# Attention products of a linear-attention and MLP kernel moved from half-array to quarter-array tiles

## The chip, the cores and the metric

The kernel runs on one core of one Trainium2 chip. The metric is device time in microseconds (us) of one execution. Every time quoted is the median of several executions of the fast state, except for two single looks (a_run, b_run32), which are called so and whose state is unknown. TensorE is called PE below, with PEld for its weight loads. VectorE is DVE, ScalarE is ACT, GpSimd is POOL, and SyncE is SP.

## The reference

A linear attention with a decaying state runs over 768 steps, for 4 batches of 8 heads of width 48. Its output, as rows of 8 x 48 = 384, goes through a layer norm and an MLP of 384 to 1536 to 384 with a residual.

```python
for t in range(S):                                    # S = 768
    cur = np.einsum('bhd,bhe->bhde', u[None] * kt, vt)
    y[:, :, t] = np.einsum('bhd,bhde->bhe', rt, state + cur)
    state = wt[:, :, :, None] * state + np.einsum('bhd,bhe->bhde', kt, vt)
x = y.transpose(0, 2, 1, 3).reshape(B, S, H * D)      # 4 x 768 x 384
xn = (x - mu) / np.sqrt(var + 1e-06) * g_ln
out = x + np.maximum(xn @ w_ch1, 0.0) @ w_ch2         # 384 -> 1536 -> 384
```

Everything is float32, except the two MLP weights, which come as float64 words that the kernel unpacks itself.

## The kernel before

The kernel works in units of two heads of one batch, 16 units in all, two units per round. Time is cut into chunks of 64 steps, and two chunks sit side by side on the 128 partitions. Within a chunk the products of R and K are built in six levels: at level `lev` only pairs of blocks of `2**lev` steps meet, and K and R are then scaled by the decays before the next level. Three kinds of product concern us: `a_ps` (R times K), `kv` (K times v, which gives the states) and `y` (A times v plus R times state). Each used the 128 rows of the array and half of its columns. To keep two heads or two chunks apart within the rows, one operand was padded with zeros (`pad`, `vz`, `s_pad`).

```python
    def right_half(q, lev):              # ACT copies R's right halves into a padded tile
        ...
        for j in range(2):
            rows = ds(HP * j, HP)
            ACT.copy(
                out=pad[rows, j, :].rearrange("p (q n) -> p q n", n=n), in_=R[rows, :, 1, :]
            )

    def level(qs, lev):
        ...
        for q in qs:
            ps = got[q] = ps_a.tile([P, NC, 2, C // 2], F32, tag="a", ...)
            for c in range(NC):
                for i in range(2):
                    m = 2 * c + i
                    PE.matmul(
                        ps[ds(C * i, C), c], st[q]["k"][:, ts(m, C)], pad[:, :, ts(m, C // 2)],
                        start=True, stop=True,
                    )
        for q in qs:
            ...   # POOL scales K, DVE scales R, then right_half(q, lev + 1) on ACT
        for q in qs:
            ...   # DVE copies the products into A under a mask
```

The MLP of a finished batch is a generator of 52 steps per batch; the schedule hands out its steps between the attention levels at a pace `RATE`.

```python
    RATE = 1.05 * MLP_STEPS * 2 / (G * NLEV)
    for rnd in range(NS + 1):
        now, old, new = ...              # the units of this round, the last and the next
        for lev in range(NLEV):
            if now:
                level(now, lev)
            if lev in (2, 3):
                for q in old[lev - 2 : lev - 1]:
                    outputs(q)
            ...                          # states, ends, loads
            if lev == 3 and old and units[old[1]][1] == G - 1:
                mlps.append(mlp(units[old[1]][0]))
            mlp_steps(RATE / 2)
            ...                          # transposes of the next units, own_term
            mlp_steps(RATE / 2)
```

Of the kernel before, what the change touches and what calls it, by code (L numbers as in the profile page):

```python
# [9 lines left out]
F32 = mybir.dt.float32  # L10
I8 = mybir.dt.int8
# [3 lines left out]
ALU = mybir.AluOpType  # L15
AX = mybir.AxisListType
PSUM = bass.MemoryType.PSUM


# [13 lines left out]
def kernel(  # L33
# [15 lines left out]
    B, H, S, D = r.shape  # L49
# [7 lines left out]
    NLEV = 6  # L57
    HALF = S // 2
    DM = H * D
# [14 lines left out]
    ps_t = ctx.enter_context(tc.tile_pool(name="ps_t", bufs=2, space=PSUM))  # L74
    ps_a = ctx.enter_context(tc.tile_pool(name="ps_a", bufs=2, space=PSUM))
    ps_y = ctx.enter_context(tc.tile_pool(name="ps_y", bufs=2, space=PSUM))
    ps_m = ctx.enter_context(tc.tile_pool(name="ps_m", bufs=2, space=PSUM))

# [8 lines left out]
    }  # L87

    vz = [const.tile([P, NC, 2, 2, D], F32, name=f"vz{i}") for i in range(2)]
    vn, xs = {}, {}  # L90

# [9 lines left out]
    def load_v(q):  # L101
        b, g = units[q]
        vn[q] = p4.tile([P, NC, 2, D], F32, tag="v", name=f"v{q}")
        for j in range(2):
            SP.dma_start(
                out=vn[q][:, :, j, :], in_=v[b, 2 * g + j].rearrange("(c p) d -> p c d", p=P)
            )

    def load_vz(q):
        b, g = units[q]  # L110
        for j in range(2):
            src = v[b, 2 * g + j].rearrange("(c p) d -> p c d", p=P)
            for i in range(2):
                rows = ds(C * i, C)
                SP.dma_start(out=vz[q % 2][rows, :, i, j, :], in_=src[rows])

# [19 lines left out]


    pads = [const.tile([P, 2, HALF], F32, name=f"pad{i}") for i in range(4)]
    a_bufs = [const.tile([P, NC, 2, C], F32, name=f"A{i}") for i in range(4)]
    s_pads = [const.tile([P, NM - 1, 2, D], F32, name=f"s_pad{i}") for i in range(1)]  # L140
    for t in (*pads, *a_bufs, *s_pads):
        DVE.memset(t, 0.0)
    for t in vz:
        POOL.memset(t, 0.0)


    masks = []
    for lev in range(NLEV - 1):
        n = 1 << lev
        m = const.tile([P, C // n, n], I8, name=f"mask2_{lev}")  # L150
        POOL.memset(m, 1.0)
        for base, sign in ((0, 1), (n - 1, -1)):
            POOL.affine_select(
                out=m, in_=m, compare_op=ALU.is_ge, fill=0.0, base=base,
                pattern=[[-2 * n * sign, C // n], [0, n]], channel_multiplier=sign,
            )
        half = const.tile([P, C // 2], I8, name=f"mask{lev}")
        m = m.rearrange("p q n -> p (q n)")
        for i in range(2):
            rows = ds(C * i, C)  # L160
            POOL.tensor_copy(out=half[rows], in_=m[rows, ds(C // 2 * i, C // 2)])
        masks.append(half.rearrange("p (q n) -> p q n", n=n))

# [89 lines left out]
    def own_term(q):  # L253
# [13 lines left out]
        DVE.tensor_reduce(out=o, in_=rk, axis=AX.X, op=ALU.add)  # L267
        a["vo"] = vn.pop(q)
        POOL.tensor_tensor(  # L269
            out=a["vo"], in0=a["vo"], in1=o[:, :, :, None].broadcast_to([P, NC, 2, D]),  # L270
            op=ALU.mult,
        )

    def right_half(q, lev):

        n = 1 << lev
        pad = pads[q % 2 * 2 + lev % 2]
        R = st[q]["r"].rearrange("p (q two n) -> p q two n", two=2, n=n)
        for j in range(2):
            rows = ds(HP * j, HP)  # L280
            ACT.copy(  # L281
                out=pad[rows, j, :].rearrange("p (q n) -> p q n", n=n), in_=R[rows, :, 1, :]
            )

    def level(qs, lev):
        n = 1 << lev
        last = lev == NLEV - 1
        got = {}
        for q in qs:
            pad = pads[q % 2 * 2 + lev % 2]  # L290
            ps = got[q] = ps_a.tile([P, NC, 2, C // 2], F32, tag="a", name=f"a_ps{q}_{lev}")
            for c in range(NC):
                for i in range(2):
                    m = 2 * c + i
                    PE.matmul(  # L295
                        ps[ds(C * i, C), c], st[q]["k"][:, ts(m, C)], pad[:, :, ts(m, C // 2)],
                        start=True, stop=True,
                    )
        for q in qs:
# [12 lines left out]
            )  # L312
            if not last:
                right_half(q, lev + 1)
        for q in qs:
            A = a_bufs[q % 4].rearrange("s c j (q two n) -> s (c j) q two n", two=2, n=n)
            ps = got[q].rearrange("s c j (q n) -> s (c j) q n", n=n)
            if last:
                for i in range(2):
                    rows = ds(C * i, n)  # L320
                    ACT.copy(out=A[rows, :, 0, 1, :], in_=ps[rows, :, 0, :])
            else:
                mask = masks[lev][:, None].broadcast_to([P, NC * 2, C // (2 * n), n])
                DVE.copy_predicated(out=A[:, :, :, 1, :], mask=mask, data=ps)  # L324

# [10 lines left out]
    def states(q):  # L336

        a = st[q]
        s = p2.tile([P, NM - 1, D], F32, tag="s", name=f"s{q}", bufs=1)
        for c0 in range(0, NC, CB):  # L340
            kv = ps_y.tile([P, CB, 2, D], F32, tag="y", name=f"kv{q}_{c0}")
            for i in range(CB):
                for j in range(2):
                    PE.matmul(  # L344
                        kv[ds(HP * j, HP), i], a["kn"][:, c0 + i, ds(HP * j, HP)],
                        vz[q % 2][:, c0 + i, :, j, :], start=True, stop=True,
                    )
            for i in range(2 * CB):
                m = 2 * c0 + i
                new = kv[:, i // 2, i % 2, :]  # L350
                if m == 0:
                    DVE.tensor_copy(out=s[:, m, :], in_=new)
                elif m < NM - 1:
                    DVE.scalar_tensor_tensor(  # L354
                        out=s[:, m, :], in0=s[:, m - 1, :], scalar=a["T"][NLEV][:, m : m + 1],
                        in1=new, op0=ALU.mult, op1=ALU.add,
                    )
        a["s"] = s_pads[0]
        for j in range(2):
            rows = ds(HP * j, HP)  # L360
            ACT.copy(out=a["s"][rows, :, j, :], in_=s[rows])  # L361

    def outputs(q):
        b, g = units[q]
        a = st.pop(q)
        if g == 0:
            xs[b] = p2.tile([P, NC, H, D], F32, tag="x", name=f"x{b}")
        for c0 in range(0, NC, CB):
            y = ps_y.tile([P, CB, 2 * D], F32, tag="y", name=f"y{q}_{c0}")
            for i in range(CB):  # L370
                c = c0 + i

                for j in range(2):
                    for half in range(2):
                        PE.matmul(  # L375
                            y[ds(C * half, C), i, ts(j, D)], a_bufs[q % 4][:, c, j, :],
                            vz[q % 2][:, c, half, j, :],
                            start=i + j == 0, stop=c + half == 0, skip_group_check=True,
                        )
                for half in range(2):  # L380
                    m = 2 * c + half
                    if m:
                        PE.matmul(  # L383
                            y[ds(C * half, C), i, :], a["r"][:, ts(m, C)],
                            a["s"][:, m - 1].rearrange("p j e -> p (j e)"),
                            start=False, stop=True, skip_group_check=True,
                        )
            DVE.tensor_tensor(
                out=xs[b][:, c0 : c0 + CB, 2 * g : 2 * g + 2, :],
                in0=y.rearrange("p c (j e) -> p c j e", j=2), in1=a["vo"][:, c0 : c0 + CB],  # L390
                op=ALU.add,
            )

# [64 lines left out]
    for q in (0, 1):  # L458
        right_half(q, 0)
        own_term(q)  # L460
# [14 lines left out]
    for rnd in range(NS + 1):  # L475
        now, old, new = ([2 * i, 2 * i + 1] if 0 <= i < NS else [] for i in (rnd, rnd - 1, rnd + 1))
        for lev in range(NLEV):
            if now:
                level(now, lev)
            if lev in (2, 3):  # L480
                for q in old[lev - 2 : lev - 1]:
                    outputs(q)
# [6 lines left out]
            if lev == 3:  # L489
                for q in now:  # L490
                    load_vz(q)
            if lev == 3 and old and units[old[1]][1] == G - 1:
                mlps.append(mlp(units[old[1]][0]))
# [9 lines left out]
            if lev == NLEV - 1:  # L503
                for q in new:
                    own_term(q)
                    right_half(q, 0)
                    if q + 2 < NU:
                        load(q + 2)
# [36 lines left out]
```

## Time and profile before

| | before |
|---|---|
| time, median of 4 runs | 707.6 us (707.15 to 708.8) |
| span of the profiled execution | 705.4 us |
| first h_ps product (start of the second stage) | 187.3 us |
| second stage, first h_ps to PE's last product | 514.7 us |
| idle time of PE in it (gaps over 0.1 us) | 10.2 us |
| time at half clock in it | 3.4 us |
| PE's instruction fetches | 43 packets |

The prediction below shows the main lines of this profile. The first fence holds, from the page, the granted clock of PE in 40 slices of the span (9 is full, 5 is half) and the queue that brings instructions. The second holds the answer for two stretches in which no MLP product runs, because one batch's MLP is finished and the next batch's has not begun. Its columns are the stretch, its length, the busy us and instructions of PE, PEld, DVE, ACT and POOL, then granted clock, DMA share and GB/s.

```profile
PEclk9665865778999999999999999999999999999999
q8 instruction: 43, 0.70, 0.4%
```

### The profile page before, as it was taken

The page shows a single profiled execution, that of the slowest core. Times are in us where ns is not written, and L with a number is a line of the kernel's source. Part 1 is how long each engine was busy: PE and PEld are TensorE (multiplying, and loading weights), DVE is VectorE, ACT ScalarE, POOL GpSimd, SP SyncE. Part 2 cuts the span into 40 slices and gives each one's busy share as a digit, 9 for nine tenths or more (in the row PEclk, how much of TensorE's full clock was granted, in tenths as well). Part 3 has the DMA queues.
Part 4 walks back from the last instruction along what each step waited for, and adds up shares of the span by engine and source line. Part 5 has one row for each costly group of instructions (what it writes and reads, how often), then busy time and mean ns, then how long its engine had stood idle before and what let it go on. Part 6 is the DMA issues. An engine that isn't in the chain of part 4 may idle for free.

```text
span 705.4 us, 13251 instructions
## 1 busy us (share of the span) xinstructions
PE 610.7 (87%) x5416; PEld 417.6 (59%) x5416; DVE 311.8 (44%) x635; ACT 279.4 (40%) x562; POOL 244.0 (35%) x303
## 2 busy tenths in 40 slices
PE   5452373677899999999999999989999999799998
PEld 4442363656556766676566666776676666455554
DVE  4779999897800532347044222573062013300000
ACT  4565574656631345335332552474133311210210
POOL 9975786887302252245023251441020100000000
PEclk9665865778999999999999999999999999999999
DMA  9908716734102440144003410030011000000000
GB/s 163 230 2 199 168 43 123 179 72 85 35 1 46 91 68 2 29 91 84 1 13 71 94 29 12 23 70 0 1 37 33 1 12 24 1 0 23 11 1 33
DMA packets 133468, 38.81 MB, mean 55 GB/s; under 512 B 127136, under 2 KB 130336, under 8 KB 133408
## 3 DMA queue, kind: packets, MB, share of 16 engines
q1 hardware_dynamic: 133408, 37.96, 26.5%
q8 instruction: 43, 0.70, 0.4%
q14 instruction: 17, 0.14, 0.1%
HBM read 33.23 MB, written 4.72 MB: 54 GB/s over the span
## 4 chain that ended last, share of the span: by engine, by line
PE 69%; DVE 16%; POOL 8%; issue 3%; ACT 3%; POOLq 0%; DVEq 0%
PE h_ps L429 27%; PE o_ps L439 25%; PE a_ps L295 7%; DVE rT L309 3%; DVE wm L212 2%; PE kv L344 2%; DVE A L324 2%; DVE wm L216 2%; PE y L383 2%; POOL tot L249 2%; PE y L375 2%; DVE we L208 1%; PE xT_ps L420 1%; ACT pad L281 1%; DVE s L354 1%
## 5 line engine op out<-in xcount | busy, mean ns | idle before, releaser
L439 PE MATMUL o_ps<-w_sb,h 128*128 128x384 f32 x576 | 192.8, 488 | 0.0
L429 PE MATMUL h_ps<-xT,w_sb 128*128 128x384 f32 x576 | 191.9, 491 | 0.3 <-ACT xT L421 0.3
L429 PEld LDWEIGHTS h_ps<-xT,w_sb 128*128 128x128 f32 x576 | 108.4, 191 | 73.3 <-issue 1.1
L439 PEld LDWEIGHTS o_ps<-w_sb,h 128*128 128x128 f32 x576 | 107.0, 190 | 69.9 <-ACT h L434 0.6
L295 PE MATMUL a_ps<-pad,kT 128*64 128x64 f32 x2304 | 100.6, 242 | 51.9 <-DVE A L324 33.3
L281 ACT COPY pad<-rT 64x384 f32<-64x384 f32 x192 | 100.0, 521 | 88.9 <-PE a_ps L295 73.9
L295 PEld LDWEIGHTS a_ps<-pad,kT 128*64 128x64 f32 x2304 | 87.8, 153 | 75.8 <-issue 37.6
L305 POOL TENSOR_TENSOR kT<-kT,tot 128x384 f32<-128x384 f32 x80 | 76.0, 964 | 158.1 <-PE a_ps L295 158.1
L445 DVE TENSOR_TENSOR o<-o_ps,x 128x384 f32<-128x384 f32 x24 | 13.4, 558 | 229.4 <-PE o_ps L439 229.4
L434 ACT ACTIVATE h<-h_ps 128x384 f32<-128x384 f32 x96 | 47.1, 490 | 125.8 <-PE h_ps L429 125.1
L324 DVE COPY_PREDICATED A<-mask,a_ps 128x384 f32<-128x384 int8 x80 | 59.1, 762 | 74.5 <-PE a_ps L295 73.5
L309 DVE TENSOR_TENSOR rT<-rT,tot 128x384 f32<-128x384 f32 x80 | 68.7, 870 | 28.9 <-ACT pad L281 28.4
L375 PE MATMUL y<-vz,A 128*64 128x48 f32 x768 | 44.3, 230 | 10.2 <-DVE s L354 10.1
L375 PEld LDWEIGHTS y<-vz,A 128*64 128x64 f32 x768 | 41.3, 148 | 13.5 <-issue 10.7
L354 DVE SCALAR_TENSOR_TENSOR s<-s,decay,kv 128x48 f32<-128x48 f32 x160 | 41.7, 261 | 4.8
L383 PE MATMUL y<-s_pad,rT 128*64 128x96 f32 x352 | 39.0, 268 | 0.9 <-ACT s_pad L361 0.9
L361 ACT COPY s_pad<-s 64x528 f32<-64x528 f32 x32 | 20.2, 630 | 45.9 <-DVE s L354 45.5
L219 POOL TENSOR_TENSOR w_sb<-wm,we 128x384 f32<-128x384 f32 x24 | 28.9, 1208 | 24.5 <-DVE wm L216 16.9
L383 PEld LDWEIGHTS y<-s_pad,rT 128*64 128x64 f32 x352 | 32.9, 148 | 1.2 <-ACT s_pad L361 1.2
L249 POOL TENSOR_TENSOR tot<-wT 128x384 f32<-128x384 f32 x16 | 13.7, 859 | 56.7 <-ACT wT L235 56.5
L305 POOL TENSOR_TENSOR kT<-kT,wT 128x384 f32<-128x384 f32 x16 | 20.2, 1276 | 32.1 <-PE a_ps L295 32.1
L269 POOL TENSOR_TENSOR v<-v,own 128x576 f32<-128x576 f32 x16 | 19.8, 1236 | 30.1 <-DMA v<-in_v_dram 30.1
(58 smaller groups left out, 544.1 us busy)
## 6 DMA issues: line engine op xcount, KB each, us to landing
raw<-in_moe_w_ch_dram SPq DMA_DIRECT2D x24, 384.0 KB, 4.9
nat_w<-in_w_dram SPq DMA_DIRECT2D x32, 144.0 KB, 3.5
nat_k<-in_k_dram SPq DMA_DIRECT2D x32, 144.0 KB, 3.9
nat_r<-in_r_dram SPq DMA_DIRECT2D x32, 144.0 KB, 4.3
v<-in_v_dram SPq DMA_DIRECT2D x32, 144.0 KB, 2.9
vz<-in_v_dram SPq DMA_DIRECT2D x64, 72.0 KB, 2.5
out_dram<-o SPq DMA_DIRECT2D x24, 192.0 KB, 1.9
u_bc<-in_u_dram SPq DMA_DIRECT2D x1, 192.0 KB, 4.3
```

The lines of the kernel that those rows point to most:

```text
L219: POOL.tensor_tensor(out=dst, in0=m, in1=e.bitcast(F32), op=ALU.mult)
L281: ACT.copy(out=pad[rows, j, :].rearrange("p (q n) -> p q n", n=n), in_=R[rows, :, 1, :])
L295: PE.matmul(ps[ds(C * i, C), c], st[q]["k"][:, ts(m, C)], pad[:, :, ts(m, C // 2)], start=True, stop=True,)
L305: POOL.tensor_tensor(out=K[:, :, 0, :], in0=K[:, :, 0, :], in1=T[:, :, 1][:, :, None].broadcast_to(blocks), op=ALU.mult,)
L309: DVE.tensor_tensor(out=R[:, :, 1, :], in0=R[:, :, 1, :], in1=T[:, :, 0][:, :, None].broadcast_to(blocks), op=ALU.mult,)
L324: DVE.copy_predicated(out=A[:, :, :, 1, :], mask=mask, data=ps)
L354: DVE.scalar_tensor_tensor(out=s[:, m, :], in0=s[:, m - 1, :], scalar=a["T"][NLEV][:, m : m + 1], in1=new, op0=ALU.mult, op1=ALU.add,)
L375: PE.matmul(y[ds(C * half, C), i, ts(j, D)], a_bufs[q % 4][:, c, j, :], vz[q % 2][:, c, half, j, :], start=i + j == 0, stop=c + half == 0, ...
L383: PE.matmul(y[ds(C * half, C), i, :], a["r"][:, ts(m, C)], a["s"][:, m - 1].rearrange("p j e -> p (j e)"), start=False, stop=True, skip_gr ...
L429: PE.matmul(ps, w1_sb[:, kc, ts(f, P)], xT[:, kc, :], start=kc == 0, stop=kc == KC - 1,)
L434: ACT.activation(out=hs[f], in_=ps, func=AF.Relu)
L439: PE.matmul(ps, hs[f][:, ts(i, P)], w2_sb[:, f, :], start=f == 0, stop=f == FC - 1)
```

## The change

The intent is to use the array in four quarters of 64 rows by 64 columns, so that two heads and two chunks run side by side, and to drop the zero padding and the copies that made it. The head sits in the rows for `a_ps` and for the state products of `y`; for the A products of `y` and for `kv` the chunk does. Where both quarters of a column half would need the same rows, a copy with its halves swapped is made (`vx`, `rx`, `sx`).

```diff
-    ps_a = ctx.enter_context(tc.tile_pool(name="ps_a", bufs=2, space=PSUM))
-    ps_y = ctx.enter_context(tc.tile_pool(name="ps_y", bufs=2, space=PSUM))
+    ps_a = ctx.enter_context(tc.tile_pool(name="ps_a", bufs=1, space=PSUM))
+    ps_y = ctx.enter_context(tc.tile_pool(name="ps_y", bufs=1, space=PSUM))
 (cut: loads, memsets and masks follow the new layout; pads, s_pads and vz go)
-    def right_half(q, lev):
 (cut)
             for c in range(NC):
                 for i in range(2):
-                    m = 2 * c + i
-                    PE.matmul(
-                        ps[ds(C * i, C), c], st[q]["k"][:, ts(m, C)], pad[:, :, ts(m, C // 2)],
-                        start=True, stop=True,
-                    )
+                    for j in range(2):
+                        m = 2 * c + i
+                        rows = ds(HP * j, D)
+                        PE.matmul(
+                            ps[ds(C * (i ^ j), C), j, u, c].rearrange("s (q n) -> s q n", n=n),
+                            K[rows, ts(m, C)], R[rows, m, :, 1, :], start=True, stop=True,
+                        )
 (cut: the same for kv and y; A is copied once per head for both units)
-            if lev in (2, 3):
-                for q in old[lev - 2 : lev - 1]:
+            if lev in (3, 4):
+                for q in old[lev - 3 : lev - 2]:
                     outputs(q)
 (cut)
-            if lev == 3 and old and units[old[1]][1] == G - 1:
+            if lev == 4 and old and units[old[1]][1] == G - 1:
                 mlps.append(mlp(units[old[1]][0]))
```

Two side effects are to be kept in mind. PE now reads R itself, where it read ACT's padded copy, so DVE may scale R only after the products. And the outputs, with the start of the next MLP, come one level later.

## The prediction

> **What bounds the kernel now.** I read the page first (engines and slices), then the table by stretches, then the chain of work that ended last, then the list of groups and the timeline of TensorE.
>
> ```profile
> PE 610.7 (87%) x5416; PEld 417.6 (59%) x5416; DVE 311.8 (44%) x635; ACT 279.4 (40%) x562; POOL 244.0 (35%) x303
> PE   5452373677899999999999999989999999799998
> DVE  4779999897800532347044222573062013300000
> ```
>
> In the slices TensorE (PE) is half idle for the first ten and full from the eleventh on. The table of two stretches, cut where the first h_ps product starts (187.4 us), has the columns: stretch, length, then busy us and instructions of PE, PEld, DVE, ACT and POOL, then granted clock, DMA share and GB/s.
>
> ```profile
> 0.00:187.40 187.40, 106.48 (x1548) 89.74 (x1549) 157.46 (x285) 109.31 (x217) 144.75 (x179) 0.75 0.62 122
> 187.40:705.40 518.00, 504.20 (x3870) 327.84 (x3868) 154.35 (x352) 170.12 (x347) 99.21 (x124) 1.00 0.14 31
> ```
>
> So there are two stages. In the first, VectorE is the busiest (157 of 187 us; 58.98 of the 60 us from 60 to 120 us in a finer cut): it unpacks the MLP weights besides its attention work. In the second, PE is busy for 504 of 518 us and nothing else comes near. The time is the start of the MLP plus all PE work still left then plus 14 us of gaps. The chain says the same of the whole span:
>
> ```profile
> PE 69%; DVE 16%; POOL 8%; issue 3%; ACT 3%; POOLq 0%; DVEq 0%
> L439 PE MATMUL o_ps<-w_sb,h 128*128 128x384 f32 x576 | 192.8, 488 | 0.0
> L429 PE MATMUL h_ps<-xT,w_sb 128*128 128x384 f32 x576 | 191.9, 491 | 0.3 <-ACT xT L421 0.3
> L295 PE MATMUL a_ps<-pad,kT 128*64 128x64 f32 x2304 | 100.6, 242 | 51.9 <-DVE A L324 33.3
> L281 ACT COPY pad<-rT 64x384 f32<-64x384 f32 x192 | 100.0, 521 | 88.9 <-PE a_ps L295 73.9
> ```
>
> The MLP (193 + 192 us) is untouched by the change. What the change can touch in the second stage is the rest of the 504 us, above all a_ps (1344 of its 2304 instructions lie there, 50.0 us by the same cut), y (29.7 and 27.7 us) and kv (15.0 us). A float32 product is two loads and two matmuls: 1152 a_ps products give x2304.
>
> How long one such instruction holds the array is read from the timeline at full clock (start, length, work; first y rows of successive blocks, then a_ps and kv bursts):
>
> ```profile
> 456.42 0.34 PE L375 MATMUL y<-vz,A 128*64 128x48 f32 x4
> ...
> 456.82 0.34 PE L375 MATMUL y<-vz,A 128*64 128x48 f32 x4
> ...
> 457.22 0.34 PE L375 MATMUL y<-vz,A 128*64 128x48 f32 x4
> ```
> ```profile
> 441.64 1.62 PE L295 MATMUL a_ps<-pad,kT 128*64 128x64 f32 x48
> 443.09 1.16 PE L344 MATMUL kv<-vz,kn 128*64 128x96 f32 x24
> 444.19 0.88 PE L333 MATMUL kn_ps<-ident,kT 128*128 128x128 f32 x6
> ```
>
> The 48 a_ps end when kv starts: 1.45 us, 24 pairs (two column halves work side by side), about 60 ns a pair, in the single starts 58. The 24 kv take 1.0 us in the chain view (0.99): 82 ns a pair. A block of y (eight of 48 columns, four of 96) comes every 0.40 us: 4t + 2 x 82 = 400 gives t = 59 ns for a pair of 48 columns. **So 64 moving columns and 48 take the same 58 ns.** The moving stream is not the floor below 64 columns[...]. In the half-clock part a 48-column pair comes every 107 ns, as a 64-column pair does: the floor scales with the array's clock, so it is in the array.
>
> [...] The change takes a_ps from 64 to 32 moving columns. The trace shows an average of 29 ns per load and matmul in a burst and nothing denser, so it neither confirms nor excludes such a floor across quarters.
>
> **The change part by part (second stage, full clock).**
> - a_ps: from 12 products of 64 columns per unit and level to 24 of 32, so 96 instructions per level of two units in place of 48. With four quarters at work: 96 / 4 x 58 ns = 1.40 us; before 48 / 2 x 58 = 1.40 us. Gain 0 over the 28 levels here (1344 / 48). [...]
> - y: per block 16 instructions (four A products, four state products, times two), each 48 columns: 4 x 58 = 233 ns in place of 400. Six blocks: 1.0 us less per unit; 12 units (576 / 48) lie here: -12 us.
> - kv: 48 instructions on four quarters, 12 x 58 = 0.70 us in place of 12 x 82 = 0.99; 11 units (264 / 24): -3.2 us.
> - Sum on PE: **-15 us** at best.
> - ACT: 192 pad copies go (100 us); 32 rx copies come (32 x 0.52 = 17 us); 32 sx copies replace the s_pad copies at an estimated 0.45 each (from 521 ns for 384 and 630 ns for 528 elements): 14 in place of 20 us. ACT falls from 279 to about 190 us; in the second stage it was 33% busy, so this is off the path.
> - DVE: the same 80 copies into A, 160 state steps and 80 rT products. Memsets fall by some 4 us, all in the first 9 us, before VectorE waits for GpSimd anyway. GpSimd loses 2 us of vz memsets, and its ten mask copies grow from 32 to 384 elements[...] in a stretch where it is on the chain.
> - DMA: vz goes from 64 to 32 transfers. It is hidden.
> - Waits: PE now reads rT itself, so VectorE's rT product must wait until a_ps has read it, where before it ran ahead behind the pad copy; and one a_ps buffer serves both units, so the next level waits for both copies into A. After a_ps that is 2 x 0.87 + 2 x 0.76 = 3.3 us. In the second stage some 9 us of MLP stand between levels (1.05 x 52 steps over 12 levels, 1.9 us each), enough to hide it. In the first, VectorE has 6.6 us of weight work per level (two parts of 3.3 us) to fill in.
> - Order: outputs move one level later and the MLP is queued a level later. In the compiled order, though, the first normalised x stands behind four rT and three A copies fewer (4 x 0.8 + 3 x 0.76 = 5.5 us of VectorE). With the new waits against it I put the first stage at -2 us net.
>
> **The rivals.**
> (1) *Quarters run four abreast*: 708 - 15 - 2 = 691 us. For it: the two column halves do so already, and the floor found scales with the array clock, so it isn't the sequencer.
> (2) *Issue becomes the bound.* Attention instructions rise from 3808 to 6848, each with a load. If a load and matmul still take 29 ns on average, a_ps becomes 96 x 29 = 2.8 us a level (+39 us), y 92 x 29 = 2.7 us a unit (+3), kv 48 x 29 = 1.4 us (+4): 708 + 46 = 754 us. The same if loads of two row quarters in one column half can't overlap. Against it: starts 7 ns apart, and a queue filled during MLP products softens it. Halfway, at 20 ns, a_ps costs +15 us and y and kv give 7 back: about 714 us.
> (3) *New waits lengthen the first stage*: rT behind a_ps, one a_ps and one y buffer. Up to 0.7 us over some 15 levels, +10 us. Against it: VectorE was 98% busy in its middle, with work to fill in.
> (4) *The first stage gets shorter by more*, with ACT 60 us lighter there: VectorE waited only 2.3 us for pads in it, so no more than about -10.
>
> **Range and chances.** Rival 1 gets 55%, around 691, with +-10 from the first stage; in-between issue rates 28%, 700 to 718; the full issue or load bound 17%, 730 to 760. The middle is 695, the range 677 to 735. 2% is 693.7 and 722: even the full PE gain only just passes it, so faster 0.44, same 0.38, slower 0.18.
>
> **What would show it.** In the changed profile: a_ps bursts of 96 near 1.5 us (right) or near 2.8 (issue or load bound); y near 1.4 us a unit, kv near 0.7; ACT near 190 us; DVE unchanged near 310; the first h_ps near 185 us; PE still over 95% busy afterwards. The prediction fails if a_ps gets clearly cheaper[...], or if the first h_ps moves by more than 10 us, or if gaps open on PE behind the single buffers.

Two steps of the forecast are estimates, which no trace showed at that time: that the 58 ns hold for quarters of 64 rows and 32 columns too, and that four quarters work side by side as two column halves do. In the trace before, the starts of two halves lie 7 ns apart and then 51, and every product takes all 128 rows. What the 58 ns consist of is not shown either; the trace shows only that 64 and 48 columns take the same time, and that it is 107 ns at half clock.

## More of the kernel before

```profile
313.00:326.50 13.50, 13.15 (x236) 10.78 (x234) 10.76 (x27) 9.61 (x22) 5.46 (x6) 1.00 0.75 137
454.00:479.00 25.00, 22.18 (x448) 18.32 (x446) 20.26 (x44) 17.45 (x36) 12.64 (x17) 1.00 0.28 58
```

The reader is to see that the clock stays full from the first h_ps product on (but for 3.4 us from 604.5 us, too short for these slices), and that even without MLP work PE was busy for 35.3 of 38.5 us: the half-array products just filled these stretches.

## The result, and the profile after

The changed kernel takes 726.5 us (median of 4 runs, 724.3 to 727.8) against 707.6 us of the kernel before on the same chip: ratio 1.0261, 95% interval 1.0233 to 1.0289. A ratio is the mean time of one kernel's fast runs over that of the other's fast runs in the same rounds, so it is not quite the ratio of the two medians. The change made the kernel slower by 2.6%, inside the predicted range but against its direction.

From the page after: engines, slices of PE and of its clock, the instruction queue, the chain that ended last, and one group, POOL's scaling of K, whose mean rose from 964 to 1128 ns.

```profile
PE 616.1 (85%) x8456; PEld 419.2 (58%) x8456; DVE 309.5 (43%) x612; ACT 190.0 (26%) x402; POOL 259.9 (36%) x301
PE   6632655568799989997999999999999999799998
PEclk9975565655799989997799999996999999999999
q8 instruction: 66, 1.08, 0.6%
PE 67%; DVE 19%; POOL 5%; issue 4%; ACT 3%; DMA 1%; POOLq 0%; SPq 0%; DVEq 0%
L296 POOL TENSOR_TENSOR kT<-kT,tot 128x384 f32<-128x384 f32 x80 | 89.3, 1128 | 207.3 <-PE a_ps L286 207.0
```

The padded copies are gone (ACT fell from 279 to 190 us, as forecast), but the clock now falls below full in several slices of the second stage, and "issue" has grown on the chain. The bursts themselves came out as forecast. From PE's timeline (start, length, work) at full clock:

```profile
429.12 1.60 PE L286 MATMUL a_ps<-rT,kT 48*64 48x32 f32 x96
430.65 1.24 PE L429 MATMUL h_ps<-xT,w_sb 128*128 128x384 f32 x3
```

A level of 96 `a_ps` matmuls takes 1.53 us (429.12 to 430.65), where the 48 halves took 1.45; 48 of `kv`, at 452.63 us in the same view, take 0.83 us (forecast 0.70). The same two stages and the two main stretches without MLP work, with the columns of the stretch table explained above:

```profile
0.00:193.20 193.20, 110.30 (x2586) 93.42 (x2586) 150.28 (x266) 70.92 (x144) 144.59 (x175) 0.67 0.60 119
193.20:724.50 531.30, 505.77 (x5873) 325.80 (x5871) 159.19 (x347) 119.10 (x259) 115.30 (x127) 0.96 0.12 26
```
```profile
328.00:349.00 21.00, 15.98 (x428) 12.91 (x426) 14.29 (x28) 8.22 (x18) 13.96 (x11) 0.70 0.37 66
478.70:499.00 20.30, 17.55 (x605) 14.81 (x605) 16.15 (x32) 8.39 (x19) 11.23 (x10) 0.78 0.12 27
```

The first h_ps comes 5.9 us later and the second stage is 13.1 us longer. PE's busy time of the second stage did not fall (504 to 506 us) although its products got shorter: the clock did that. In the two dry stretches PE is now idle for 7.8 of 41.3 us, and the granted clock is 0.70 and 0.78 in place of 1.00. The chain of work through the first of them (start, length, what) runs like this:

```profile
330.55 2.97 DMA nat_r<-in_r_dram
...
333.87 1.42 POOL rk L256
...
336.79 0.04 DVE own L265
...
337.46 0.75 DVE x L388
...
338.20 1.24 DVE rT L300
...
341.95 2.34 PE a_ps L286 x74
```

From 330.55 to 341.95 us nothing on the chain is PE's: a load of r, POOL's and DVE's work for the next unit's own product, the addition into x, DVE's scaling of R, and (cut) copies of R and four copies into A on ACT. PE's gaps in these 11 us are 0.73, 1.47, 2.60 and 0.22 us long; the second is a wait for issue (see the next list), the others are for copies into A and for POOL's scaling of K. What PE waited for in the second stage, from 193 us on (engine, line, releaser, total us, times, longest):

```profile
PE xT_ps L420 <- DVE xn L412: 4.2, 1, 4.2
PE kn_ps L330 <- POOL kT L296: 4.1, 2, 2.6
PE y L382 <- issue: 3.0, 2, 2.2
PE w_ps L229 <- ACT wT L233: 2.9, 3, 1.0
PE y L372 <- issue: 2.7, 2, 1.5
PE a_ps L286 <- issue: 1.5, 1, 1.5
```

Here 7.2 us are waits for nothing that the profile shows ("issue"). The kernel before has no such wait of 0.3 us or more in its second stage. Waits of `a_ps` for the copies into A, that is for its single buffer, come to only 0.9 us (not shown). The waits for issue all lie inside long dense runs of quarter products: four of the five in the `y` of a run of 96 `a_ps` followed at once by 92 `y`, the fifth after 65 further `a_ps`. They are 7.2 of the 11.7 us by which PE's idle time grew, and two of them (1.47 us at 335.1, 1.25 us at 486.3 us) lie in the two stretches without MLP work.

**An account of the second stage.** From the traces I took the idle time of PE, and half of PE's busy time at half clock (what a full clock would have saved, as the same `a_ps` pair takes 15 ns at full and 28 ns at half clock in the run a_run below). What is left is the work itself at full clock. Each row is one profiled execution; the last rows are experiments told below.

| kernel | first h_ps | second stage | idle of PE | half-clock time | lost to it | left |
|---|---|---|---|---|---|---|
| before | 187.3 | 514.7 | 10.2 | 3.4 | 1.5 | 503.0 |
| after | 193.2 | 527.8 | 21.9 | 44.2 | 20.1 | 485.9 |
| before, pace 0.95 | 187.4 | 506.7 | 7.3 | 0.0 | 0.0 | 499.4 |
| after, pace 0.95 | 191.9 | 508.5 | 16.3 | 15.8 | 6.7 | 485.5 |
| before, three edits | 187.4 | 506.3 | 2.4 | 2.0 | 1.0 | 502.9 |
| after, three edits | 187.2 | 502.0 | 7.5 | 15.1 | 6.6 | 487.9 |

In the last column the quarters save 17.0, 13.8 and 15.0 us (from unrounded values): the forecast gain of 15 us on the array is there. It was overpaid by 11.7 us of idle time, 18.5 us of half clock and 5.9 us of first stage: -17.0 + 11.7 + 18.5 + 5.9 = 19.1 us, and the spans differ by 19.1. The column is a remainder, so that sum closes by construction; what speaks for it is that three pairs give a similar saving.

### The profile page after: what moved, and what is told of

It reads as the page before. It is cut to its first block, busy times and chain, and to the rows that moved or that the text cites. A ratio compares the mean times of both kernels' runs of the same rounds, so it can differ in the third digit from the quotient of the medians.

```text
span 724.5 us, 18947 instructions
## 1 busy us (share of the span) xinstructions
PE 616.1 (85%) x8456; PEld 419.2 (58%) x8456; DVE 309.5 (43%) x612; ACT 190.0 (26%) x402; POOL 259.9 (36%) x301
## 3 DMA queue, kind: packets, MB, share of 16 engines
q8 instruction: 66, 1.08, 0.6%
## 4 chain that ended last, share of the span: by engine, by line
PE 67%; DVE 19%; POOL 5%; issue 4%; ACT 3%; DMA 1%; POOLq 0%; SPq 0%; DVEq 0%
PE h_ps L429 25%; PE o_ps L439 23%; PE a_ps L286 9%; DVE rT L300 3%; DVE A L313 3%; DVE we L206 2%; DVE s L351 2%; PE xT_ps L420 2%; DVE wm L210 2%; DVE wm L214 2%; PE y L372 2%; DVE we L198 1%; DVE we L203 1%; PE y L382 1%; ACT A L311 1%
## 5 line engine op out<-in xcount | busy, mean ns | idle before, releaser
L439 PE MATMUL o_ps<-w_sb,h 128*128 128x384 f32 x576 | 193.3, 488 | 0.0
L296 POOL TENSOR_TENSOR kT<-kT,tot 128x384 f32<-128x384 f32 x80 | 89.3, 1128 | 207.3 <-PE a_ps L286 207.0
L286 PE MATMUL a_ps<-rT,kT 48*64 48x32 f32 x4608 | 106.3, 247 | 58.3 <-DVE A L313 39.8
L286 PEld LDWEIGHTS a_ps<-rT,kT 48*64 48x64 f32 x4608 | 97.6, 166 | 83.9 <-issue 57.8
L358 ACT COPY sx<-s 64x288 f32<-64x288 f32 x32 | 13.7, 430 | 100.3 <-DVE s L351 100.0
L372 PE MATMUL y<-v,A 64*64 64x48 f32 x384 | 26.9, 232 | 6.5 <-DVE s L351 5.3
L233 ACT COPY rT<-r_ps 128x384 f32<-128x384 f32 x32 | 13.9, 480 | 66.4 <-PE r_ps L229 41.7
L372 PEld LDWEIGHTS y<-v,A 64*64 64x64 f32 x384 | 24.7, 146 | 8.2 <-issue 8.2
L256 POOL TENSOR_TENSOR rk<-nat_k,nat_r 128x576 f32<-128x576 f32 x16 | 23.3, 1458 | 16.8 <-PE a_ps L286 8.2
L372 PE MATMUL y<-vx,A 64*64 64x48 f32 x384 | 26.3, 232 | 1.5 <-issue 1.5
L421 ACT ACTIVATE xT<-xT_ps,g_sb 128x384 f32<-128x384 f32 x24 | 13.1, 578 | 54.7 <-PE xT_ps L420 54.6
L342 PE MATMUL kv<-v,kn 64*64 64x48 f32 x768 | 19.6, 246 | 9.2 <-DVE s L351 5.4
```

The lines of the kernel that those rows point to most:

```text
L256: POOL.tensor_tensor(out=rk, in0=nat["k"][q % 2][:, :, :, 0:D], in1=nat["r"][q % 2][:, :, :, 0:D], op=ALU.mult,)
L286: PE.matmul(ps[ds(C * (i ^ j), C), j, u, c].rearrange("s (q n) -> s q n", n=n), K[rows, ts(m, C)], R[rows, m, :, 1, :], start=True, stop=True,
L296: POOL.tensor_tensor(out=K[:, :, 0, :], in0=K[:, :, 0, :], in1=T[:, :, 1][:, :, None].broadcast_to(blocks), op=ALU.mult,)
L342: PE.matmul(kv[ds(HP * j, HP), i, c], a["kn"][ds(C * i, C), c, ds(HP * j, HP)], vn[q][ds(C * i, C), c, j, :], start=True, stop=True,)
L372: PE.matmul(y[ds(C * i, C), j, c], A[rows, j, q % 2, c, :], vx[q][rows, c] if j else vn[q][rows, c, j], start=c == 0, stop=c + i == 0, ski ...
L439: PE.matmul(ps, hs[f][:, ts(i, P)], w2_sb[:, f, :], start=f == 0, stop=f == FC - 1)
```

## The experiments

Four theories were to be told apart. **T1**: dense runs of quarter products use up instructions faster than they are fetched. **T2**: where one batch's MLP is finished and the next has not begun, the other engines' chain sets the time, PE's shorter work leaves it idle, and its clock falls. **T3**: the lost decoupling (R read by PE itself, single buffers) lengthens the first stage. **T4**: quarter products keep the array so little occupied that the clock falls even without idle time. All 18 kernels gave correct results. Ratios are to the kernel before in the same rounds (707.1 to 707.7 us); ratios are given where three rounds were run.

### Pace of the MLP: a_rate95, b_rate95, a_rate90, b_rate90 (T2)

```diff
-    RATE = 1.05 * MLP_STEPS * 2 / (G * NLEV)
+    RATE = 0.95 * MLP_STEPS * 2 / (G * NLEV)
```

A lower pace leaves MLP steps over for the batch change. First the changed kernel:

> The kernel after, with the MLP spread at 0.95 of its even rate in place of 1.05, so that each batch's MLP still has work when the next batch's x is finished. Theory 'batch change': the two stretches of some 20 us without MLP work (328 to 349 and 479 to 499 us) and their half-clock lapses (17 and 14 us) go: 12 to 22 us less, 704 to 714 us. Theory 'instruction supply': the gaps inside runs stay, at most 2 us from them. Theory 'lost decoupling': no change beyond 2 us.

Measured: 707.2 us, ratio 0.9993 (0.9978 to 1.0008), 19 us less than after. One stretch without MLP products over 8 us is left, 11.6 us long at 330 us, where after had four; half-clock time fell from 44.2 to 15.8 us. The clock in the page (40 slices, as above):

```profile
PEclk8555555555699999999799999999999999999999
```

T2 holds for the larger part, but the edit is not clean: the waits for issue fell with it, from 7.2 to 3.3 us, though they had been expected to stay. The control is the same edit in the kernel before:

> The kernel before with its MLP pace lowered from 1.05 to 0.95, the edit that brought the changed kernel from 726.5 to 707.2 us. If the loss is that the changed kernel runs out of MLP work at the two batch changes (where the kernel before lost little: one lapse of the clock of 3.4 us in the second stage), this edit has little to win here: 700 to 707 us, at most 7 us below 707.6. Rival: the pace was badly set for both kernels, and the edit takes 12 to 20 us from the kernel before as well (688 to 696 us); then the pace explains nothing of the change's loss.

Measured: 699.1 us, ratio 0.9887 (0.9872 to 0.9902). Both expectations missed: the kernel before gains 8 us, a little more than the first allowed (7) and less than the rival said (12 to 20). So pace 1.05 was not the best for either form, and of the 19 us that it gives the changed kernel only 11 belong to the change. At like pace the changed kernel is still 8 us behind.

> The changed kernel at pace 0.90. With 0.95 one stretch without MLP products was left (11.6 us at 330 us) and 15.8 us at half clock. If running dry is the loss, both go: 701 to 705 us. Rival: too slow a pace leaves MLP work for the end, where it has no other work beside it: 708 to 716 us.

Measured: 702.3 us (697.9 to 703.2, a wider spread than usual), ratio 0.9916 (0.9882 to 0.9950). As T2 expected, no dry stretch over 8 us remains, though 12.5 us at half clock and 14.4 us of idle do.

> The kernel before at pace 0.90. At 0.95 it never ran dry, so a lower pace has nothing more to win: 698 to 703 us. If it is below 697 us, 0.95 was not its best pace and the like-paced comparison must use this one.

Measured: 701.1 us, ratio 0.9918 (0.9892 to 0.9944). It is within the expectation: 0.95 was about the best pace for the halves.

### The first stage: a_pin, a_dec (T3)

In the changed kernel, DVE's reduction for the next unit's own product stands ahead of the last addition into x, and it waits for POOL, which waits for a late load. The first experiment holds it behind that addition.

```diff
+        if last_x:
+            with tc.issue_after(last_x[-1]):
+                DVE.tensor_reduce(out=o, in_=rk, axis=AX.X, op=ALU.add)
+        else:
             DVE.tensor_reduce(out=o, in_=rk, axis=AX.X, op=ALU.add)
 (cut: last_x collects the additions into x)
```

> The kernel after, with one ordering added on VectorE: the own-term reduction of the units to come may not go ahead of the last x addition of the units that finish. Theory 'batch change' (the second x of a batch stands in VectorE's queue behind that reduction, which waits for GpSimd and a late load; TensorE runs out of MLP work and its clock is halved): the stretch without MLP work shrinks by 4 to 5 us at each of three batch changes and the clock lapses of 17 and 14 us shrink with it, 10 to 20 us in all, 706 to 716 us. Theory 'instruction supply' (dense runs of quarter products outrun the fetching of instructions): the five gaps of 0.8 to 2.2 us inside y and a_ps runs stay, no change beyond 2 us. Theory 'lost decoupling' (rT waits for a_ps now): no change beyond 2 us.

Measured: 719.0 us, ratio 1.0159 (1.0133 to 1.0185): 7.5 us less than after, a miss (706 to 716 us was expected). The first h_ps came at 187.8 in place of 193.2 us, but the dry stretches stayed (20.7 and 24.0 us), with 42.5 us at half clock. The edit was meant for the batch change and worked on the first stage instead.

```diff
-            R = st[q]["r"].rearrange("p (m q two n) -> p m q two n", m=NM, two=2, n=n)
+            R = st[q]["r"].rearrange("p (q two n) -> p q two n", two=2, n=n)
+            rh = p2.tile([P, S // 2], F32, tag="rh", name=f"rh{q}_{lev}")
+            ACT.copy(out=rh.rearrange("p (q n) -> p q n", n=n), in_=R[:, :, 1, :])
 (cut: the products read rh; one v buffer fewer to make room)
```

> The kernel after, but a_ps reads a copy of the right half of rT made by ScalarE (96 copies of 128x384, about 46 us more on ScalarE), as the kernel before read its pads; the products stay in quarters; one v buffer fewer pays for it. Theory 'lost decoupling': the first MLP product returns from 193 to about 187 us and waits of VectorE for a_ps in the first stage go: 6 to 12 us less, 714 to 720 us. Theories 'instruction supply' and 'batch change': no gain beyond 3 us, the gaps inside the y runs stay.

Measured: 723.0 us, ratio 1.0211 (1.0195 to 1.0226), less gain than expected. Its first h_ps came at 188.4 us, and the second stage was 529.3 us, 1.5 longer than after, so part of it was given back. Two different edits each bring the first stage back, so its loss is shown to be avoidable, but which of the two orders caused it is not settled. It is not chance: the first h_ps lies at 185.6 to 187.8 us in all five changed kernels with the pin and their own order of outputs, and at 191.8 to 193.3 us in the changed kernel and the five variants of it with neither the pin nor the copy (a_rate95, a_rate90, a_fill, a_run, a_sched).

### Supply of instructions: a_fill, a_run, b_run32 (T1, T4)

```diff
             if now:
                 level(now, lev)
+            mlp_steps(RATE / 3)
 (cut: the two other mlp_steps(RATE / 2) become mlp_steps(RATE / 3))
```

> The kernel after, with a third of a level's MLP steps put between the a_ps products and the y, kv or kn products of the same level, so that no run of quarter products is longer than about 100. Theory 'instruction supply': the gaps with no other waiting reason inside y and a_ps runs (2.2, 0.8, 1.5, 1.25 and 1.5 us, 7.2 in all) go away, and with them the half-clock lapse of 6.8 us at 261 us: 7 to 11 us less, 716 to 720 us. Theories 'batch change' and 'lost decoupling': within 2 us of 726.

Measured: 720.9 us, ratio 1.0190 (1.0175 to 1.0205), a gain of 5.6 us. MLP products, with few instructions per us (576 `o_ps` matmuls with their loads keep PE busy for 193.3 us in the page after, 0.34 us each, where a quarter pair takes 15 ns), now stand between `a_ps` and `y`. The waits put down to issue fell from 7.2 to 2.9 us and the lapse of the clock at 261 us vanished, as T1 expected. The direct test is a dense run that waits for no data:

```diff
-            for c in range(NC):
+            for c in [c for _ in range(8 if qs[0] == 8 and lev == 2 else 1) for c in range(NC)]:
```

> The changed kernel with the A products of two units at one level issued 8 times (the result stays right), one unbroken run of 768 quarter products that wait for no data. Instruction supply: the run stalls again and again, with gaps of 0.5 to 2 us put down to issue, about one for each 256 instructions of 16 KB, and lasts 14 to 18 us in place of 8 x 1.5 = 12 us. Rival (the 0.8 to 2.2 us gaps in dense stretches are a wait for data or a buffer that the profile does not name): no gaps, 12 to 12.5 us.

Measured, one look (744.1 us). PE's timeline in the run, with the idle time ahead of a row and its releaser in brackets:

```profile
305.87 4.16 PE L286 MATMUL a_ps<-rT,kT 48*64 48x32 f32 x271
311.27 2.06 PE L286 MATMUL a_ps<-rT,kT 48*64 48x32 f32 x128 [1.24 <-issue]
314.72 10.48 PE L286 MATMUL a_ps<-rT,kT 48*64 48x32 f32 x369 [1.39 <-issue]
```

The same stretch by windows, with the columns explained above (the clock is the number after POOL's):

```profile
306.00:312.00 6.00, 4.76 (x322) 4.65 (x322) 0.00 (x0) 0.00 (x0) 1.31 (x5) 1.00 0.06 18
312.00:318.00 6.00, 4.61 (x216) 4.50 (x212) 0.56 (x1) 0.00 (x0) 1.28 (x1) 0.64 0.02 5
318.00:324.00 6.00, 5.91 (x224) 5.77 (x219) 0.00 (x0) 0.00 (x0) 0.00 (x0) 0.50 0.02 5
```

The run lasts 19 us, not 12. It first goes at about 15 ns per load and matmul (4.16 us for 271) and then stalls twice, with exactly 128 matmuls, that is 256 instructions with their loads, between the two stalls. In the instruction queue, 16 KB packets start at 308.63 and 312.41 us; PE stops 1.4 and 0.9 us after these starts and goes on 2.6 and 2.3 us after them. So 256 instructions came in 3.45 us (311.27 to 314.72), 27 ns per pair, when the array could take one in 15. At 313.6 us, 0.3 us into the second stall, the clock falls to half. From then on the pairs take 28 ns (10.48 us for 369), and there are no more stalls in the run: at half speed the supply keeps up.

The counts of the two pages agree with 256 instructions in each packet of 16 KB (66 packets are 1.08 MB): after, PE's 8456 loads and 8456 matmuls are 16,912 = 66.1 x 256, and the queue moved 66 packets; before, 10,832 = 42.3 x 256 and 43 packets.

The next experiment runs halves of 32 columns. A pair of `kv` with 96 columns took 82 ns in the trace before, so 32 columns would fill an estimated 27 of the 58 ns of a pair.

```diff
+            for c in [c for _ in range(8 if qs[0] == 8 and lev == 2 else 0) for c in range(NC)]:
+                for i in range(2):
+                    m = 2 * c + i
+                    PE.matmul(
+                        ps[ds(C * i, C), c, 0], st[q]["k"][:, ts(m, C)],
+                        pad[:, 0, ts(m, C // 2)], start=True, stop=True,
+                    )
```

> The kernel before with 8 more passes of half-array products of only 32 moving columns at the same unit and level (their results are overwritten or not read, so the output stays right): dense, without waits, about 768 products at near 29 ns[...], some 22 us. If products[...] count as little activity (T4), the granted clock falls to half during or just after this run. If the lapses follow idle time of PE alone, there is no lapse here, the clock stays at 1.00.

Measured, one look (717.6 us). I had miscounted the run: it holds 432 matmuls, not 768 (384 of 32 moving columns and the level's own 48 of 64), and lasts 12.8 us, so 29.7 ns each. The start of it in PE's timeline, then two windows of the run:

```profile
303.12 5.79 PE L295 MATMUL a_ps<-pad,kT 128*64 128x32 f32 x192
308.74 0.90 PE L302 MATMUL a_ps<-pad,kT 128*64 128x64 f32 x24
```
```profile
302.00:308.00 6.00, 6.00 (x172) 5.26 (x170) 0.00 (x0) 0.00 (x0) 0.81 (x4) 1.00 0.01 3
308.00:314.00 6.00, 6.00 (x213) 6.00 (x210) 1.14 (x2) 1.02 (x2) 0.92 (x1) 1.00 0.01 3
```

There is no gap and no lapse: the clock is 1.00 throughout 12.8 us of products nearly all of only 32 moving columns. T4 falls for half-array products of that width, and that was its main argument. For quarters no run was made, but the kept traces say more. In every trace the clock changes only at steps of 3.41 us, so it can be read window by window. At full clock quarters alone did not lower it: in a_run from 306.80 to 310.22 us PE was busy for 3.23 of 3.42 us and the clock stayed; in the next window it was busy for 2.06 of 3.41 us, and the clock fell. At half clock, though, quarters did not bring it back. The first line below is the third window of a_run at half clock with only quarters and hardly a gap, and the clock stayed at half after it, as after the one before; the second is the window of MLP products that was followed by full clock. The third line is the kernel before, busy at half clock with attention halves alone, just before its clock went to full at 126.66 us.

```profile
320.46:323.87 3.41, 3.31 (x128) 3.18 (x124) 0.00 (x0) 0.00 (x0) 0.00 (x0) 0.50 0.02 5
327.28:330.70 3.42, 3.42 (x6) 1.90 (x7) 2.72 (x11) 0.32 (x1) 0.00 (x0) 0.50 0.02 5
```
```profile
123.25:126.66 3.41, 3.41 (x59) 3.41 (x57) 1.11 (x3) 0.00 (x0) 3.32 (x2) 0.50 0.80 302
```

Over the 20 traces, I counted the windows at half clock in which PE was busy for over 90% and no other products than halves, or than quarters, started: full clock followed after 18 of 18 with halves and after 5 of 21 with quarters. So T4 survives in another form: the clock falls in stretches with idle time, and quarters then keep it down longer. How much of the half-clock time this makes was not separated, and no run was made to test it.

The packets of instructions come here at 306.70, 310.47 and 314.25 us, one for each 3.8 us, and PE never stops: the halves use instructions just about as fast as the stalled quarters got them.

### The order of outputs: a_sched, a_sched_pin_rate

```diff
-            if lev in (3, 4):
-                for q in old[lev - 3 : lev - 2]:
+            if lev in (2, 3):
+                for q in old[lev - 2 : lev - 1]:
                     outputs(q)
 (cut: the MLP is queued at lev == 3 in place of 4)
```

> The changed kernel with its outputs, and with them the start of the next batch's MLP, one level earlier, as in the kernel before (levels 2 and 3 in place of 3 and 4). If the stretches without an MLP product at the two batch changes (20.9 and 20.5 us) are long because the MLP starts one level later, they shrink by some 5 us each and the lapses there shorten: 716 to 722 us against 726.5. Rival: the length of these stretches is set by the other engines' chain (r transposes, own product, scaling of R and K, the last addition into x), and the y products now come before their states and copies are ready: the stretches stay near 20 us and the time is 725 to 735 us.

Measured: 722.7 us (720.1 to 726.3), ratio 1.0220 (1.0183 to 1.0257). The time lies between the two expectations. The dry stretches are 17.2 and 24.8 us where they were 20.9 and 20.5, so the rival is right about them: the later outputs are not what makes them long. The few us gained are within this kernel's own spread.

> The same earlier outputs together with the pinned own reduction and pace 0.95. If all three are gains: 695 to 700 us, the first kernel with quarters at or below the like-paced kernel before (699.1). If the earlier outputs cost: 704 to 712 us.

Measured: 706.3 us, ratio 0.9983 (0.9964 to 1.0002). That is in the range of the second expectation, but its reading, that the earlier outputs cost, does not follow: the same two edits without the earlier outputs (a_pin_rate, run later, below) take 710.5 us. Its first h_ps came at 193.6 us in spite of the pin, where a_pin_rate has 185.6, with 27.3 us at half clock around the change of stage, and its second stage is shorter (507.1 against 518.4 us); why the pin does not work with the earlier outputs was not looked into.

### The edits together: a_pin_fill_rate, a_pin_rate, a_pin_rate90, a_pin_fill_rate90

> The changed kernel with the three edits that each helped: own reduction of the next unit held behind the last addition into x (7.5 us alone), MLP steps between the A products and the y products of a level (5.6 us alone), pace 0.95 (19.3 us alone). If first stage, dense quarter runs and batch changes are separate losses, the gains add up in part (first stage 5 us, stalls of the dense runs 4 us, on top of 707): 696 to 700 us, first h_ps near 188 us, gaps of PE in the second stage near 12 us, under 15 us at half clock. Rival: all three work on the same loss, and the sum is no better than pace alone: 704 to 708 us.

Measured: 702.2 us, ratio 0.9932 (0.9915 to 0.9948), 5 us below pace alone, above the first expectation and below the rival's. The first h_ps came at 186.5 us as expected. Dry stretches of 11.4 and 13.1 us, with 25.3 us at half clock, had come back.

> The changed kernel with the pinned own reduction and pace 0.95, without the fill (all three gave 702.2 us, with lapses of the clock at 256 and 335 us). If the fill caused these lapses, by spending MLP steps earlier in a level: 697 to 701 us and less than 15 us at half clock in the second stage. If the fill was a gain: 703 to 707 us.

Measured: 710.5 us, ratio 1.0041 (1.0024 to 1.0059), worse than pace 0.95 alone (707.2) and than both expectations. The first h_ps is 6.3 us earlier (185.6) and the second stage 9.9 us longer (518.4), with 29.4 us at half clock and two dry stretches. An MLP that starts earlier at the same pace also ends earlier, while the next batch's attention is not ready earlier, so the saved time turns into a dry stretch. That reading was argued from these two traces and not tested by itself.

> The changed kernel with the pinned own reduction and pace 0.90 (pace 0.90 alone gave 702.3, its first stage 192.2 us). If the first stage is a separate loss that the pin removes, 696 to 699 us with the first h_ps near 187.5 us and the second stage near 505 us: the quarters then just beat the halves at their own best pace (699.1). Rival: the gain of the first stage is given back in the second, 701 to 704 us.

Measured: 705.2 us (699.4 to 707.2), ratio 0.9956 (0.9910 to 1.0002). It is 1 us above the rival's range, and its runs spread. The rival's reading fits: against pace 0.90 alone the first h_ps comes 5.0 us earlier (187.2 against 192.2) and the second stage is 8.1 us longer (513.0 against 504.9).

> The same with the fill between A products and y products. If instruction supply still costs 4 to 7 us of gaps put down to issue at pace 0.90, the fill takes 3 us or more off: 693 to 697 us. If the gaps of the dense runs are by then hidden or replaced by others: the same as without the fill, within 2 us.

Measured: 693.7 us (692.7 to 694.8), ratio 0.9807 (0.9788 to 0.9825), the fastest of all kernels here and 11.5 us below the same without the fill. That is more than the waits for issue alone, which were 3.1 us there: half-clock time fell too, from 25.4 to 15.1 us, and idle time from 17.5 to 7.5. PE's waits from 193 us on, the whole list down to 0.6 us, and its second stage by windows:

```profile
PE kn_ps L335 <- POOL kT L301: 3.4, 1, 3.4
PE a_ps L291 <- ACT A L316: 1.6, 1, 1.6
PE a_ps L291 <- DVE s L354: 1.0, 1, 1.0
PE xT_ps L426 <- DVE o L451: 0.6, 2, 0.3
```
```profile
187.20:692.70 505.50, 494.49 (x5871) 317.45 (x5869) 163.25 (x353) 118.43 (x259) 121.09 (x132) 0.99 0.12 27
```

No wait for issue is left, and PE's busy time of the second stage is 494 us where after had 506. In the page the clock is at 9 in every slice from the seventeenth on.

### The same edits for the halves: b_pin_rate, b_fill_rate95, b_pin_fill_rate90

> The kernel before with pace 0.95 and the pinned own reduction. The pin was worth 5 us of first stage in the changed kernel, where DVE's queue is longer there; the first stage of the kernel before has no such delay (187.4 us), so it should win nothing here: 698 to 700 us (699.1 with pace alone). Rival: the pin is a general gain: 692 to 696 us, and then it says nothing of the change.

Measured: 703.4 us, ratio 0.9939 (0.9919 to 0.9958), against 0.9887 with pace alone. The pin costs the kernel before 4 us, outside both expectations; its first h_ps came at 190.5 us. So the pin is no general gain.

> The kernel before at its best pace so far, 0.95, with MLP steps also between the A products and the rest of a level. Halves consume instructions at half the quarters' rate and showed no stalls in dense runs, so if the fill works by relieving the supply of instructions it gives nothing here: 698 to 701 us. Rival: the fill is a better mix of work for any form: 691 to 696 us, and the quarters have no gain of their own.

Measured: 702.1 us, ratio 0.9928 (0.9900 to 0.9955). The fill gives the halves nothing, as T1 expected, and costs a little more than the range allowed.

> The kernel before with exactly the three edits of the changed kernel at 693.7 us. The pin cost it 4 us at pace 0.95: 699 to 705 us, that is 6 to 11 us above the quarters, against 15 us of the array's forecast gain less a longer lapse of the clock early in the second stage. Rival: 693 to 696 us, no gain of the quarters.

Measured: 700.9 us, ratio 0.9904 (0.9883 to 0.9926). With exactly the same three edits the quarters are 7.2 us faster (693.7), by the two ratios 0.9807 / 0.9904 = 0.990. Against the best form of the halves that was tried (pace 0.95 alone, 699.1 us; fewer were tried than of the quarters) they are 5.5 us faster, 0.9807 / 0.9887 = 0.992. So the change is a gain of about 1% once the schedule is made for it, and a loss of 2.6% as it was made.

## Why the prediction was wrong, step by step

- **The floor of 58 ns and a_ps, gain 0: right.** 1.53 us per level where MLP products follow (1.42 at the median of the 21 whole levels at full clock) against 1.40 forecast and 1.45 before. That the 58 ns of the trace hold for 64 rows and 32 columns was an estimate: 1.53 us for 96 over four quarters are 64 ns in each, and the 29.7 ns of b_run32 over two halves, nearly all of 32 columns, are 59 ns in each.
- **y and kv, -15 us in sum: right.** The work left in the account falls by 17.0, 13.8 and 15.0 us in three like-treated pairs; kv at 0.83 us was somewhat above its 0.70, and 92 `y` took 1.52 us a unit against 1.40. ACT at 190 us and DVE at 309.5 us came as forecast, and rival 1's step, four quarters abreast, holds for short bursts (96 in 1.53 us, one every 16 ns).
- **"... plus all PE work still left then plus 14 us of gaps", kept for the changed kernel because "some 9 us of MLP stand between levels ..., enough to hide it": this is the step that failed.** The 9 us are an average. At the two batch changes there is no MLP for some 20 us each, and there the time is set by the chain of the other engines, which the change did not shorten. PE's idle time went from 10.2 to 21.9 us (7.2 of it the waits for issue below). Pace 0.95, which moves MLP work into these stretches, took 11 us more from the changed kernel than from the kernel before.
- **The clock was taken as full ("second stage, full clock"), with no reason given.** This is the other half of the same step: every product was put at full clock. Half-clock time rose from 3.4 to 44.2 us, worth 18.5 us, the largest term of the loss. In the second stages of all traces (their last 8 us left out) each of the 40 falls of the clock followed a window of 3.41 us with 0.9 us or more of idle PE, but 55 other such windows, with up to 1.6 us, had no fall. Every kernel here with less idle time in its second stage than after also had less half-clock time, though not in proportion: a_sched had more idle time (25.5 us) and less of it (35.4 us). Quarters that keep the clock down (a_run, and the count told there) are likely another part.
- **Rival 2 was put as a steady rate, but the supply acts in runs.** "A queue filled during MLP products softens it" was right for a burst of 96 (1.53 us; in a_run 271 matmuls went before the first stall) and wrong for `a_ps` and `y` back to back. 7.2 us of waits for issue came of it, which stand in the windows before three of the four lapses of the clock after the change of stage (at 261, 336 and 490 us); only the first lapse went away with a_fill, which left 2.9 us of these waits. a_run showed the stalls alone.
- **First stage, -2 us: wrong, +5.9.** Rival 3 had the direction and somewhat more than half of the size. Two different edits remove it.
- **"Gaps open on PE behind the single buffers"**, named as what would make the forecast fail, hardly happened in the second stage: `a_ps` waited 0.9 us for the copies into A. The gaps opened elsewhere.
- **The chances.** Even without the failed steps the forecast could not reach 2% surely, and the slower side got 0.18 because the loss was sought in the array and in issue only, not in what PE would wait for when its work got shorter.

What stays open: the exact rule by which the clock falls and comes back; why the pin costs the halves 4 us and does not bring the first stage back with the earlier outputs; which of two orders made the first stage longer; and what the single buffers cost there, as they were not doubled again in any run.

## What to carry to other kernels

When the work of the bounding engine gets shorter, look for the stretches where it was only just the bound: the gain turns into idle time there, and on PE idle time can cost again as much through the clock (11.7 us of it came here with 18.5 us of half clock). Ask not only how long a smaller tile takes but how many instructions per us it uses: mix dense runs of small products with products that use few. Compare two forms of a kernel at a schedule tuned for each, as the one on which the old form was tuned holds a handicap for the new one.

## What the runs showed of the hardware

- **Supply of instructions.** 256 of PE's instructions came in 3.45 us when they were the bound (a_run), and PE stood for 1.24 and 1.39 us in its two stalls. Dense quarter products (15 ns per load and matmul) outran this supply there, while half-array products (29.7 ns in b_run32) did not.
- **Quarters side by side.** A load and matmul of halves took 29 ns on average. In a burst of 96 quarters one came every 16 ns over all quarters (1.53 us / 96), 64 ns in each.
- **The clock.** The lapses in the second stage of the changed kernel are multiples of 3.41 us long (3.4 to 17.1 us). In a_run the clock fell at 313.6 us after a gap of PE of 1.24 us and the first 0.3 us of one of 1.39, 1.35 us of idle time within 3.41 us; and a busy PE stayed at half clock from 314.7 to 327.3 us with quarters. The kernel before had gaps of 1.15 us at most, 2.8 us in sum, over the 25 us from 454 us on, and no lapse.
- **POOL beside DVE.** After the change POOL's scaling of K and DVE's scaling of R are both released by the same products, and the mean of the POOL instruction rose from 964 to 1128 ns with shapes unchanged. In the trace after, 56 of its 80 instructions overlap such a DVE instruction, with a median of 1182 ns, and the 24 that do not have 904; before, only 24 overlap (1019 ns), and the other 56 have 879. So the slower ones go with the overlap; the cause is not shown, and no run tested it alone.
